# Keeping the first batch's u only transposed, and ending on column halves of the last chunk: an attention and mixer kernel on one core

## The chip, the cores and the metric

One core of a Trainium2 chip. The metric is the device time of one execution in microseconds (us). A profiled execution has a span, from first to last instruction record, some 1.8 us shorter than its device time; "span" below always means that one. All executions that are compared here counted as fast. A few of them, of the kernel before too, still took 1 to 4 us more than the rest; the two of which a trace was taken (named below) show TensorE at half clock for some 7 us near the beginning. Medians are quoted for that reason.

## The reference

Eight batches. Attention of 8 heads over 576 tokens of width 64, causal by blocks of 64; its output x has 512 columns. A mixer follows: token mixing with a hidden width of 256, then channel mixing with a hidden width of 1536.

```python
x = attention(q, k, v).transpose(0, 2, 1, 3).reshape(B, S, H * D)   # 8 x 576 x 512
xt = x.transpose(0, 2, 1)
h = np.maximum(xt @ w_tok1, 0.0) @ w_tok2
u = x + h.transpose(0, 2, 1)
h2 = np.maximum(u @ w_ch1, 0.0) @ w_ch2
return (u + h2).astype(np.float32)
```

## The kernel before

Work is handed to a planner: each `P.add(engine, cost, emit, deps, prio)` is one operation, and the planner simulates the engines and fixes the order on each by priorities and estimated readiness. So a change in one place moves instructions elsewhere. Matmul outputs live in four banks named `mm`; attention scores have two double banks of their own, `sc`. `EVAC` means "VectorE or ScalarE, as the planner likes".

The 576 tokens of a batch are four chunks of 128 rows and one of 64. The 64-row chunks of two batches share one "mixed" chunk (`um`). u is made in row layout, and is also needed transposed (uT) as the channel-up matmuls' moving operand. The first batch gets its uT directly, by a separate function, early; its u in row layout is then computed a second time, only because the output needs it:

```python
    def token_mix(b, x_done, w1_ready, w2_ready):
        # ... for b == 0 uT comes from first_uT(...)
        for si in range(5):
            # emit: two matmuls of 512 columns, w2_sb against aT       (L782)
            op = P.add("PE", mm_cost(512, 2), emit, ..., take=[(BANK, bank)])
            # emit: u = bank + x, or um for si == 4                     (L803)
            op = P.add("DVE", dve_cost(512), emit, [op], prio, give=[bank])
            u_done.append(op)
```

Channel-down makes the output chunk by chunk, and a last mixed chunk of its own kind ends the kernel:

```python
    def last_down(gt, ut, deps, prio):
        bank = {}
        def emit(o):
            nc.tensor.matmul(out=bank_of(bank), lhsT=ident, rhs=ut, start=True, stop=False)   # adds u
            for cc in range(NDC):                                                             # NDC = 12
                nc.tensor.matmul(out=bank_of(bank), lhsT=gt[:, cc, :], rhs=wc2_sb[:, cc, :],
                                 start=False, stop=(cc == NDC - 1))
        # ...
        for f, engine in enumerate(EVAC):          # one half of the columns on each engine, same bank
            def emit(o, f=f):
                cols = slice(256 * f, 256 * f + 256)
                cast(o, o_sb[oi][:, 0, cols], bank_of(bank)[:, cols])
            halves.append(P.add(engine, evac_cost(256)[engine], emit, [op] + o_war, prio))
        for kk in range(2):                        # 64 rows each, one on SyncE's queue, one on ScalarE's
            # dma_start(out=out[B - 2 + kk, 512:576, :], in_=o_sb[oi][64 * kk : 64 * kk + 64, 0, :])
            P.add(("SP", "ACT")[kk], 0.5, emit, halves, prio, xfer=4 * 0.086)

    def channel_down(b, g_done, wc2_ready, u_done, prio, mixed=False):
        # ... the last batch's mixed chunk: return last_down(...)
        for n, si in enumerate(chunks):
            for part in range(3):                  # four matmuls of 512 columns each
                deps = [prev] + (g_done + wc2_ready + u_done + o_war if part == 0 else [])
                # ...
            # VectorE: o_sb = bank + u ; every second chunk one store of 256 rows, 512 KB
```

The softmax here doesn't subtract the row's maximum and nothing guards it: scores larger than these inputs give would overflow.

## Time and profile before

| | before |
|---|---|
| device time, median of 6 (range) | 312.94 us (312.66 to 314.96) |
| span of the profiled execution | 311.63 us |
| first channel-up matmul starts | 29.89 us |
| last matmul ends | 306.30 us |
| last store issued | 307.20 us |
| its landing | 309.82 us |
| TensorE's idle time from 30 to 300 us | 1.49 us |

The middle rows come from the single records of the trace. Together they cut the span into parts that can be added: what comes before the first channel-up matmul, the middle up to the last matmul, and four steps of the end. The page, the chain, the groups and the order of time at the end are shown in the prediction. Two more views are used later. The first is the table by stretches, whose columns are the stretch, its length, the busy time (and instructions) of TensorE, its weight loads, VectorE, ScalarE and GpSimd, then clock, DMA share and GB/s:

```profile
40.00:50.00 10.00, 10.00 (x115) 5.03 (x112) 6.34 (x15) 6.48 (x8) 6.01 (x8) 1.00 1.25 200
60.00:70.00 10.00, 9.31 (x153) 5.39 (x152) 7.51 (x16) 6.87 (x11) 1.65 (x4) 1.00 1.40 182
```

TensorE has no gap at all from 40 to 50 us, and 0.69 us of gap from 60 to 70. The second is the list of stores issued after 305.5 us (tile, engine, count, size, median us from issue to landing):

```profile
out_dram<-o_sb SPq DMA_DIRECT2D x1, 128.0 KB, 2.3
out_dram<-o_sb ACTq DMA_DIRECT2D x1, 128.0 KB, 2.6
```

### The profile page before, as it was taken

How to read it: one execution, taken by the hardware profiler on the slowest of the kernel's cores; microseconds unless marked ns; L12 is line 12 of the kernel's file. 1: busy time of each engine (PE TensorE's matmuls, PEld its weight loads, DVE VectorE, ACT ScalarE, POOL GpSimd, SP SyncE). 2: the span in 40 equal slices, each digit the busy share in tenths (PEclk: the TensorE clock that was granted, in tenths of full speed). 3: DMA queues.
4: the chain of work that ended last, by engine and by line, in shares of the span. 5: the costliest groups of instructions: out<-in, count | busy, mean ns of one | idle time of the engine just before them, and what ended most of it. 6: DMA issues, size and time to landing. Idle time of an engine off the chain costs nothing.

```text
span 311.6 us, 7140 instructions
## 1 busy us (share of the span) xinstructions
PE 302.3 (97%) x3010; PEld 154.7 (50%) x3010; DVE 159.4 (51%) x377; ACT 164.8 (53%) x234; POOL 63.1 (20%) x96
## 2 busy tenths in 40 slices
PE   8999999999999999999999999999999999999993
PEld 3574436455465554554554555544444644444641
DVE  6868748598795495678375644452033021011021
ACT  5885862769756746677655475315505404604400
POOL 7956435711611501500400000000000000000000
PEclk9999999999999999999999999999999999999998
DMA  7999999997993996971690112114311313011013
GB/s 234 195 197 207 222 210 183 223 186 106 123 168 56 145 152 141 143 47 33 64 135 33 38 30 40 69 67 53 67 67 68 69 67 103 0 67 68 2 67 102
DMA packets 56864, 33.13 MB, mean 106 GB/s; under 512 B 43840, under 2 KB 47296, under 8 KB 56832
## 3 DMA queue, kind: packets, MB, share of 16 engines
q0 software_dynamic: 36960, 18.52, 45.5%
q1 hardware_dynamic: 19504, 13.44, 16.7%
q10 hardware_dynamic: 368, 0.72, 0.6%
q8 instruction: 23, 0.38, 0.5%
q14 instruction: 9, 0.07, 0.1%
HBM read 35.85 MB, written 9.44 MB: 145 GB/s over the span
## 4 chain that ended last, share of the span: by engine, by line
PE 83%; DMA 5%; DVE 5%; POOL 3%; issue 2%; ACT 0%; POOLq 0%
PE mm L979 29%; PE mm L874 27%; PE sc L460 7%; PE mm L507 7%; PE mm L688 5%; PE mm L782 4%; PE mm L901 4%; DMA qraw<-in_q_dram 3%; DMA kraw<-in_k_dram 2%; DVE x_sb L535 1%; DVE u_sb L803 1%; POOL gT L378 1%; PE mm L931 1%; POOL wc_sb L416 1%; POOL w_sb L397 1%
## 5 line engine op out<-in xcount | busy, mean ns | idle before, releaser
L479 ACT ACTIVATE e_sb<-sc 128x1024 bf16<-128x1024 f32 x95 | 92.5, 1027 | 37.7 <-PE sc L460 36.8
L979 PE MATMUL mm<-wc_sb,gT 128*128 128x512 bf16 x384 | 89.1, 379 | 0.0
L874 PE MATMUL mm<-uT,wc_sb 128*128 128x512 bf16 x384 | 88.4, 379 | 0.2 <-DVE x_sb L535 0.2
L674 ACT ACTIVATE gT<-mm 128x512 bf16<-128x512 f32 x74 | 44.2, 597 | 60.4 <-PE mm L874 60.3
L995 DVE TENSOR_TENSOR o_sb<-mm,u_sb 128x512 f32<-128x512 f32 x32 | 22.1, 690 | 87.1 <-PE mm L979 87.0
L874 PEld LDWEIGHTS <-wc_sb 128*128 128x128 bf16 x384 | 36.2, 98 | 45.3 <-issue 4.0
L979 PEld LDWEIGHTS <-gT 128*128 128x128 bf16 x384 | 35.3, 98 | 42.5 <-issue 4.3
L460 PE MATMUL sc<-qT,kT 32*128 32x320 bf16 (+4 forms) x744 | 35.9, 281 | 0.9 <-DVE qT L349 0.8
L507 PEld LDWEIGHTS <-e_sb 128*128 128x128 bf16 x896 | 31.1, 97 | 9.6 <-issue 4.6
L507 PE MATMUL mm<-v,e_sb 128*128 128x65 bf16 x896 | 33.2, 193 | 1.4 <-DVE uT L852 0.7
L378 POOL DMA_DIRECT2D v<-in_v_dram x30 | 25.4, 866 | 30.5 <-PE mm L507 27.9
L535 DVE TENSOR_TENSOR x_sb<-mm,rinv 128x320 bf16<-128x320 f32 x64 | 30.5, 489 | 1.4
L803 DVE TENSOR_TENSOR u_sb<-mm,x_sb 128x512 bf16<-128x512 f32 x32 | 20.1, 684 | 8.9 <-PE mm L782 8.1
L676 DVE TENSOR_SCALAR gT<-mm 128x512 bf16<-128x512 f32 x22 | 15.1, 688 | 15.3 <-PE mm L874 15.3
L460 PEld LDWEIGHTS <-kT 32*128 32x128 bf16 x752 | 12.7, 93 | 19.8 <-issue 17.0
L349 DVE STREAM_TRANSPOSE kT<-kraw 128x576 int32<-128x576 int32 (+1 forms) x20 | 20.1, 1033 | 4.5 <-PE sc L460 3.4
L349 DVE STREAM_TRANSPOSE qT<-qraw 128x576 int32<-128x576 int32 (+1 forms) x20 | 19.9, 1020 | 0.8 <-DMA qraw<-in_q_dram 0.5
L782 PE MATMUL mm<-aT,w_sb 128*128 128x512 bf16 x80 | 19.2, 379 | 0.0
L688 PE MATMUL mm<-x_sb,w_sb 128*128 128x512 bf16 (+1 forms) x102 | 17.9, 316 | 0.3 <-DVE x_sb L535 0.3
L674 ACT ACTIVATE aT<-mm 128x512 bf16<-128x512 f32 (+1 forms) x17 | 9.3, 547 | 16.7 <-PE mm L688 16.5
L329 POOL DMA_DIRECT2D kraw<-in_k_dram x15 | 8.4, 563 | 42.2 <-DVE kT L349 29.9
L485 DVE MEMSET e_sb<- 64x128 uint32 (+1 forms) x72 | 10.6, 153 | 11.2 <-ACT e_sb L479 8.0
(70 smaller groups left out, 183.9 us busy)
## 6 DMA issues: line engine op xcount, KB each, us to landing
out_dram<-o_sb SPq DMA_DIRECT2D x16, 512.0 KB, 2.8
kraw<-in_k_dram POOLq DMA_DIRECT2D x15, 288.0 KB, 6.6
qraw<-in_q_dram POOLq DMA_DIRECT2D x15, 288.0 KB, 7.7
v<-in_v_dram POOLq DMA_DIRECT2D x24, 128.0 KB, 5.3
wc_sb<-in_moe_w_ch_dram POOLq DMA_DIRECT2D x8, 192.0 KB, 8.0
wc_sb<-in_moe_w_ch_dram POOLq DMA_DIRECT2D x3, 512.0 KB, 10.7
gT<-in_v_dram POOLq DMA_DIRECT2D x9, 128.0 KB, 6.2
gT<-in_v_dram POOLq DMA_DIRECT2D x4, 256.0 KB, 12.9
```

The lines of the kernel that those rows point to most:

```text
L349: nc.vector.transpose(dst[:, 0:S, :] .rearrange("p s e -> p (s e)") .bitcast(I32) .rearrange("p (a k) -> p k a", k=NB)[:, k0:k1], raw2.bit ...
L378: nc.gpsimd.dma_start(out=dst, in_=src)
L460: nc.tensor.matmul(out=home(n)[:, c0 : c0 + w], lhsT=kT[i][r, j0 : j0 + 128, par], rhs=qT[i][r, i0 : i0 + w, par], start=(par == 0), stop= ...
L479: nc.scalar.activation(dst, sc[SC.index(note["pool"])][:, :, 0:n], EXP, scale=scale)
L507: nc.tensor.matmul(out=u[:, I, 0:65], lhsT=w, rhs=vt[:, J, head, 0:65], start=(J == 0), stop=(J == I),)
L535: nc.vector.tensor_tensor(out=xt[:, :, 64 * head : 64 * head + 64], in0=u[:, :, 0:64], in1=ri.to_broadcast([128, 5, 64]), op=MULT,)
L674: nc.scalar.activation(dst, src, RELU)
L688: nc.tensor.matmul(out=bank_of(bank)[:, w * n : w * n + w], lhsT=wt[:, 128 * tt : 128 * (tt + 1)], rhs=xt[:, c, cols], start=(c == 0), sto ...
L782: nc.tensor.matmul(out=bank_of(bank), lhsT=w2_sb[:, t, c0 : c0 + 128], rhs=at[:, t, :], start=(t == 0), stop=(t == NDT - 1),)
L803: nc.vector.tensor_tensor(out=dst, in0=bank_of(bank)[r, :], in1=xt[r, si, :], op=ADD)
L874: nc.tensor.matmul(out=bank_of(bank), lhsT=wc1_sb[:, m, 128 * cc : 128 * (cc + 1)], rhs=uT[b % 2][:, :, m, :], start=(m == 0), stop=(m == ...
L979: nc.tensor.matmul(out=bank_of(bank), lhsT=gt[:, cc, c0 : c0 + 128], rhs=wc2_sb[:, cc, :], start=(cc == 0), stop=(cc == NDC - 1),)
```

## The change

Two ideas. The first batch's row-layout u for its four full chunks isn't computed; in channel-down each output bank is opened by four 128-column matmuls that turn uT back (uT as weights, the identity as moving operand), the twelve ordinary ones accumulate on top, and the addition becomes a plain copy that either engine may do. At the end, the mixed chunk becomes an ordinary one and goes ahead of the last batch's regular chunks; the third regular chunk is stored by itself, and the fourth is computed, added and stored in two column halves, each in its own bank. On the way the wait for a free output tile moved from the matmuls to the evacuation.

```diff
-        for si in range(5):
+        for si in range(4 if b == 0 else 0, 5):
...
-    def last_down(gt, ut, deps, prio):          # all of it goes
...
+        turned = b == 0 and not mixed
+            last = b == B - 1 and n == 3
+            paired = not mixed and not (b == B - 1 and n >= 2)
+            for cols in (slice(0, 256), slice(256, 512)) if last else (slice(0, 512),):
...
+                        for m in range(NDM) if turned and part == 0 else ():
+                            nc.tensor.matmul(out=ps[:, 128 * m : 128 * (m + 1)],
+                                lhsT=uT[b % 2][:, si, m, :], rhs=ident, start=(m == 0), stop=False)
                         for cc in range(4 * part, 4 * part + 4):
-                            nc.tensor.matmul(out=bank_of(bank), ..., rhs=wc2_sb[:, cc, :], start=(cc == 0), ...)
+                            nc.tensor.matmul(out=ps, ..., rhs=wc2_sb[:, cc, cols], start=(cc == 0 and not turned), ...)
-                deps = [prev] + (g_done + wc2_ready + u_done + o_war if part == 0 else [])
+                    deps = [prev] + (g_done + wc2_ready + u_done if part == 0 else [])
...
+                    if turned:
+                        cast(o, dst, ps)
+                    else:
+                        nc.vector.tensor_tensor(out=dst, in0=ps, in1=..., op=ADD)
+                if not mixed and not paired:
+                        nc.sync.dma_start(out=out[b, c0 : c0 + 128, cols], in_=o_sb[oi][:, n % 2, cols])
...
+            if p == B - 1:       # after the mixed chunk, whose priority is now 10 * p + 3.9
+                channel_down(p, g_done, wc2_ready, u_done, 10 * p + 4)
```

More of the change, by code (lines that the diff above doesn't have):

```diff
@@ L858, in token_mix @@
         if not odd:
-            um_first[pair] = [u_done[4]]
+            um_first[pair] = [u_done[-1]]
         return done, um_done, u_done
@@ L922 @@
     out_n = [0]
-    def last_down(gt, ut, deps, prio):
-        bank = {}
-        def emit(o):
-            nc.tensor.matmul(out=bank_of(bank), lhsT=ident, rhs=ut, start=True, stop=False)
-            for cc in range(NDC):
-                nc.tensor.matmul(
-                    out=bank_of(bank),
-                    lhsT=gt[:, cc, :],
-                    rhs=wc2_sb[:, cc, :],
-                    start=False,
-                    stop=(cc == NDC - 1),
-                )
-        op = P.add(
-            "PE", mm_cost(512, NDC + 1), emit, deps + pads["ident"], prio, take=[(BANK, bank)]
-        )
-        oi = out_n[0] % 3
-        o_war = reuse(("o", oi))
-        halves = []
-        for f, engine in enumerate(EVAC):
-            def emit(o, f=f):
-                cols = slice(256 * f, 256 * f + 256)
-                cast(o, o_sb[oi][:, 0, cols], bank_of(bank)[:, cols])
-            halves.append(P.add(engine, evac_cost(256)[engine], emit, [op] + o_war, prio))
-        for kk in range(2):
-            def emit(o, kk=kk):
-                queue = nc.sync if o.engine == "SP" else nc.scalar
-                queue.dma_start(
-                    out=out[B - 2 + kk, 512:576, :],
-                    in_=o_sb[oi][64 * kk : 64 * kk + 64, 0, :],
-                )
-            P.add(("SP", "ACT")[kk], 0.5, emit, halves, prio, xfer=4 * 0.086)
     def channel_down(b, g_done, wc2_ready, u_done, prio, mixed=False):
@@ L964, in channel_down @@
         ut = um_sb[b // 2 % 2] if mixed else u_sb[b % 3]
-        if mixed and b == B - 1:
-            return last_down(gt, ut, g_done + wc2_ready + u_done, prio)
+        turned = b == 0 and not mixed
+        prev = None
         for n, si in enumerate(chunks):
-            bank = {}
-            prev = None
+            c0 = 0 if mixed else 128 * si
+            last = b == B - 1 and n == 3
+            paired = not mixed and not (b == B - 1 and n >= 2)
             if n % 2 == 0:
@@ L974, in channel_down @@
                 halves = []
-            c0 = 0 if mixed else 128 * si
-            for part in range(3):
-                def emit(o, part=part, c0=c0, bank=bank):
-                    for cc in range(4 * part, 4 * part + 4):
-                        nc.tensor.matmul(
-                            out=bank_of(bank),
-                            lhsT=gt[:, cc, c0 : c0 + 128],
-                            rhs=wc2_sb[:, cc, :],
-                            start=(cc == 0),
-                            stop=(cc == NDC - 1),
-                        )
-                deps = [prev] + (g_done + wc2_ready + u_done + o_war if part == 0 else [])
-                prev = P.add(
-                    "PE", mm_cost(512, 4), emit, deps, prio + 0.1 * n - 0.01 * part,
-                    take=[(BANK, bank)] if part == 0 else (),
-                )
@@ L992, in channel_down @@
-            reads(("gm", b // 2 % 2) if mixed else ("g", b % 2), prev)
-            def emit(o, si=si, oi=oi, n=n, bank=bank):
-                nc.vector.tensor_tensor(
-                    out=o_sb[oi][:, n % 2, :],
-                    in0=bank_of(bank),
-                    in1=ut if mixed else ut[:, si, :],
-                    op=ADD,
-                )
-            op = P.add("DVE", dve_cost(512), emit, [prev] + u_done, prio, give=[bank])
-            reads(("um", b // 2 % 2) if mixed else ("u", b % 3), op)
@@ L1004, in channel_down, with emit @@
-            halves.append(op)
+            for cols in (slice(0, 256), slice(256, 512)) if last else (slice(0, 512),):
+                width = cols.stop - cols.start
+                bank = {}
+                if paired or mixed:
+                    prev = None
+                for part in range(3):
+                    def emit(o, part=part, si=si, c0=c0, cols=cols, width=width, bank=bank):
+                        ps = bank_of(bank)[:, 0:width]
+                        for m in range(NDM) if turned and part == 0 else ():
+                            nc.tensor.matmul(
+                                out=ps[:, 128 * m : 128 * (m + 1)],
+                                lhsT=uT[b % 2][:, si, m, :],
+                                rhs=ident,
+                                start=(m == 0),
+                                stop=False,
+                            )
+                        for cc in range(4 * part, 4 * part + 4):
+                            nc.tensor.matmul(
+                                out=ps,
+                                lhsT=gt[:, cc, c0 : c0 + 128],
+                                rhs=wc2_sb[:, cc, cols],
+                                start=(cc == 0 and not turned),
+                                stop=(cc == NDC - 1),
+                            )
+                    deps = [prev] + (g_done + wc2_ready + u_done if part == 0 else [])
+                    cost = mm_cost(width, 4) + (mm_cost(128, 4) if turned and part == 0 else 0)
+                    prev = P.add(
+                        "PE", cost, emit, deps, prio + 0.1 * n - 0.01 * part + cols.start * 1e-4,
+                        take=[(BANK, bank)] if part == 0 else (),
+                    )
+                reads(("gm", b // 2 % 2) if mixed else ("g", b % 2), prev)
+                if turned:
+                    reads(("uT", b % 2), prev)
+                def emit(o, si=si, oi=oi, n=n, cols=cols, width=width, bank=bank):
+                    dst, ps = o_sb[oi][:, n % 2, cols], bank_of(bank)[:, 0:width]
+                    if turned:
+                        cast(o, dst, ps)
+                    else:
+                        nc.vector.tensor_tensor(
+                            out=dst, in0=ps, in1=(ut if mixed else ut[:, si, :])[:, cols], op=ADD
+                        )
+                op = P.add(
+                    EVAC if turned else "DVE", evac_cost(width), emit, [prev] + u_done + o_war, prio, give=[bank]
+                )
+                reads(("um", b // 2 % 2) if mixed else ("u", b % 3), op)
+                halves.append(op)
+                if not mixed and not paired:
+                    def emit(o, oi=oi, n=n, c0=c0, cols=cols):
+                        nc.sync.dma_start(out=out[b, c0 : c0 + 128, cols], in_=o_sb[oi][:, n % 2, cols])
+                    P.add("SP", 0.5, emit, [op], prio, xfer=8 * 0.086 * width / 512)
@@ L1013, in channel_down @@
                     reads(("o", oi), P.add("SP", 0.5, emit, halves, prio, xfer=4 * 0.086))
-            elif n % 2 == 1:
+            elif paired and n % 2 == 1:
                 def emit(o, oi=oi, i0=128 * (n - 1)):
@@ L1047 @@
             g_done = channel_up(p, uT_done, wc1_ready, 10 * p + 2)
-            channel_down(p, g_done, wc2_ready, u_done, 10 * p + 4)
+            if p < B - 1:
+                channel_down(p, g_done, wc2_ready, u_done, 10 * p + 4)
             if p % 2 == 1:
                 gm_done = channel_up_mixed(p // 2, um_done, wc1_ready, 10 * p + 3.5)
-                channel_down(p, gm_done, wc2_ready, u_done, 10 * p + 5, mixed=True)
+                prio = 10 * p + (5 if p < B - 1 else 3.9)
+                channel_down(p, gm_done, wc2_ready, u_done, prio, mixed=True)
+            if p == B - 1:
+                channel_down(p, g_done, wc2_ready, u_done, 10 * p + 4)
     with tc.manual_schedule():
```

## The prediction

> **What bounds the kernel now.** I read the page first (engines, slices, groups), then the chain of waits, the table by stretches of 10 us, the waits of TensorE, and last the order of time of the final 10 us.
>
> ```profile
> span 311.6 us, 7140 instructions
> PE 302.3 (97%) x3010; PEld 154.7 (50%) x3010; DVE 159.4 (51%) x377; ACT 164.8 (53%) x234; POOL 63.1 (20%) x96
> PE   8999999999999999999999999999999999999993
> PEclk9999999999999999999999999999999999999998
> GB/s 234 195 197 207 222 210 183 223 186 106 123 168 56 145 152 141 143 47 33 64 135 33 38 30 40 69 67 53 67 67 68 69 67 103 0 67 68 2 67 102
> ```
>
> TensorE has work in 97% of the span, in every slice but the first and last, at full clock. The 9.3 us in which it has none (311.6 - 302.3) split, by the stretches of 10 us, into 2.15 us before 20 us, 1.86 us between 20 and 300 us, and 5.3 us after the last matmul. So time comes off in three ways only: fewer columns through TensorE, fewer of those 1.86 us, or a shorter end. The loads are busy for the first 70 us, where VectorE is also most loaded: it is there that an earlier TensorE could run into something.
>
> The price of a matmul is read from the chain of waits, where long runs stand without a gap (start us, us, what), not from the mean durations of the groups, which overlap:
>
> ```profile
> 223.02 10.36 PE mm L979 x48
> 243.74 2.68 PE mm L901 x48
> ```
>
> 512 columns: 10.36 / 48 = 0.216 us each. 128 columns: 2.68 / 48 = 0.056 us each. The groups, with shapes kept apart, give the other durations (us busy, then mean ns of one):
>
> ```profile
> L782 PE MATMUL mm<-aT,w_sb 128*128 128x512 bf16 x80 | 19.2, 379 | 0.0
> L835 PE MATMUL mm<-ident,u_sb 128*128 128x128 bf16 x16 | 1.3, 220 | 0.0
> L803 DVE TENSOR_TENSOR u_sb<-mm,x_sb 128x512 bf16<-128x512 f32 x32 | 20.1, 684 | 8.9 <-PE mm L782 8.1 <-issue 0.8
> L995 DVE TENSOR_TENSOR o_sb<-mm,u_sb 128x512 f32<-128x512 f32 x32 | 22.1, 690 | 87.1 <-PE mm L979 87.0
> ```
>
> Last, the end, in order of time:
>
> ```profile
> 303.33 0.38 PE L929 MATMUL mm<-um_sb,ident 128*128 128x512 bf16 x1
> 303.55 2.75 PE L931 MATMUL mm<-wc_sb,gmT 128*128 128x512 bf16 x12
> 303.59 0.69 DVE L995 TENSOR_TENSOR o_sb<-mm,u_sb 128x512 f32<-128x512 f32 x1 [0.17 <-PE mm L979]
> 306.33 0.37 ACT L309 COPY o_sb<-mm 128x256 f32<-128x256 f32 x1 [12.57 <-PE mm L931]
> 306.74 0.42 DVE L311 COPY o_sb<-mm 128x256 f32<-128x256 f32 x1 [2.46 <-ACT o_sb L309]
> 307.19 0.47 SPq L954 DMA_DIRECT2D out_dram<-o_sb  x1
> 307.20 0.55 ACTq L954 DMA_DIRECT2D out_dram<-o_sb  x1
> ```
>
> The kernel meant the two copies to run side by side on two engines; they run one after the other, 0.86 us from the first start to 307.19. Both stores wait for both. From their issue to the end of the span it is 311.6 - 307.19 = 4.4 us.
>
> **What the Trainium skill says.** (1) "TensorE: Matmul & The Clock Gate", section "Back-to-back issue gap", gives N/2.4 + 2.5 ns for warm back-to-back matmuls, but also says that real streams of weight load and matmul settle elsewhere: about 81 ns at 128 columns and 131 ns at 512. This trace sides with the formula: 0.056 and 0.216 us, weight loads included, so the trace's numbers are used. (2) "PSUM — Partial Sum Buffer", section "Terms", says that two engines on one bank and quadrant at once is an error, reads against reads included. That is why the two end copies, halves of one bank, are kept apart: VectorE's shows an idle time ended by ScalarE. The changed kernel gives each column half its own bank. (3) "DMA: Bandwidth & Descriptors", section "Anatomy of one DMA — SWDGE (gpsimd) path", puts a nearly constant 2.0 us on a transfer, mostly the write's receipt. Written for another issuing path, it fits here: 128 KB stores issued from SyncE take a median of 2.4 us to land. So the end cannot fall much below its 4.4 us by moving fewer bytes.
>
> **The change, part by part.**
>
> First batch. The four 128-row chunks of u in row layout are no longer computed: 4 x 2 = 8 matmuls of 512 columns go, 8 x 0.216 = 1.73 us of TensorE, and 4 additions on VectorE of 0.684, 2.7 us. In exchange each output bank is opened by four matmuls of 128 columns, the transposed u against the identity: 16 x 0.056 = 0.89 us. They use the accumulation that the bank does anyway, so nothing else is added. Net on TensorE: -0.84 us. The four output additions (0.69 on VectorE) become plain copies; in the changed program's order one lies on VectorE and three on ScalarE (0.60 each, by the mean of ScalarE's 128x512 evictions), so VectorE loses 4 x 0.684 + 3 x 0.69 = 4.8 us of work between 28 and 70 us, and ScalarE gains 1.8.
>
> End. The mixed chunk goes in among the regular ones as an ordinary chunk: 12 matmuls as before, without the one that added u by the identity: -0.22 us. Its two stores go out some microseconds before the end. The last regular chunk is 24 matmuls of 256 columns, which at half of 0.216 each is the same 2.6 us. After the last matmul there is one 256-column addition on VectorE; at the 0.42 us of the 256-column copy, against 0.86 for the two in a row: -0.43 us. Then one store of 128 KB in rows of 1 KB in place of two of 128 KB. The end's 256 KB showed 133 and 129 GB/s in the two microseconds from 308 us, so about 2 us of moving; half of that with the fixed part unchanged I put at -0.2 us, an estimate, not -1.
>
> Waits between 20 and 300 us. The largest is this:
>
> ```profile
> PE mm L507 <- DVE uT L852: 0.7, 1, 0.7
> ```
>
> It is at 67.6 us: VectorE, behind four additions, a fifth and a transpose, empties a bank late. In the changed order four transpose matmuls and four of the output's stand between that point and the attention of the next batch, and VectorE carries less. I expect this wait to go, and something smaller to come elsewhere: -0.4 us of the 1.86, with an error as large as that.
>
> Sum: -0.84 - 0.22 - 0.43 - 0.2 - 0.4 = -2.1 us. From the median of 312.9: **310.8 us**, 0.7% faster.
>
> **The rivals.**
>
> A. The loads set the pace early, and what TensorE saves is waited away. For it: some 200 GB/s (195 to 234 by slice) through the first 45 us; GpSimd waits there for landings of weights and v; the second batch's last cast of v ends at 47.05 us and attention on TensorE starts at 48.26, only 1.2 us later, while the change moves TensorE forward by 1.73 - 0.45 = 1.28 us by then (eight of the sixteen small matmuls come earlier). Against it: VectorE's casts at 45.59 us came after a fill that waited for ScalarE's exponentials, not for a load, and that fill moves forward too. If v lands no earlier, 0.1 to 1 us is lost: 311 to 312 us.
>
> B. The scheduler's new order makes new bank waits. The order of all instructions differs from 28 us on, and a bank that waits for the last of several evictions on one engine costs 0.2 to 0.7 us each time, as it does at 68 and 70 us in this trace. Three extra copies on ScalarE stand ahead of exponentials around 50 to 70 us, where it is 41% to 85% busy by stretch. Two or three such waits would cost 1 us: 311.5 to 312. Against it: the waits are few even where VectorE is 88% busy, and that load falls.
>
> C. The bigger prize: VectorE's relief in the crowded stretch takes out nearly all of the 1.86 us, and the store at the end shrinks by a full microsecond: 308.8. Against it: the fixed part of a store, and most of the waits lying outside the first two batches' output.
>
> D. The end grows: four stores now leave SyncE in the last few microseconds, and the last ones queue behind a 512 KB one. Against it: before, 512 KB issued at 304.31 was moved by 307. In the new order the 512 KB leave about 1.5 us sooner, and the two halves' stores are 1.3 us apart, twice an issue. I give it +0.3 us at most.
>
> **Range and chances.** Only the 1.06 us of TensorE work are nearly sure. Each of the other terms could fail by its own size, rival A and B can cost 1 us together, C can give 1.5, and the three runs before spread from 312.66 to 314.96. So 309.5 to 312.4 should hold it 8 times in 10. Over 2% faster means below 306.7, more than TensorE's columns, all its waits and any shortening of the end that I can argue for add up to: 2%. Over 2% slower would need 6 us of new waits: 2%. Within 2%: 96%.
>
> **What would show it.** TensorE's busy time falls from 302.3 to about 301.2. The new identity matmuls are 16, of 128 columns, and the group of u against w_sb falls from 80 to 72. In the waits of TensorE, the 0.7 us for uT is gone and the sum from 20 to 300 us is about 1.5 us; well over 2 is rival B, and waits for casts of v or for transposes of q and k near 46 us are rival A. At the end, one VectorE addition of 0.42 us lies between last matmul and last store, and last matmul to end of span is about 4.7 us in place of 5.3. The prediction is wrong in kind if TensorE gains its 1.06 us and the time stays at 312.9: the saving was then waited away in the first 70 us, or the clock fell.

## The result, and the profile after

Changed kernel: 310.74 us median of 6 (310.42 to 311.1); before, in the same rounds, 312.94. Ratio 0.9921, interval [0.9898, 0.9944]. Ratios here are the mean time of one kernel's fast runs over that of the other's of the same rounds, so not quite the ratio of the medians that are quoted. 310.8 had been predicted. The agreement is worth little by itself: the parts of the sum have to be compared.

The page of the changed kernel:

```profile
span 309.2 us, 7176 instructions
PE 300.4 (97%) x3029; PEld 155.4 (50%) x3029; DVE 157.6 (51%) x372; ACT 165.8 (54%) x235; POOL 63.1 (20%) x96
PE   7999989999999999999999999999999999999995
PEclk9999999999999999999999999999999999999999
```

TensorE lost 1.9 us of busy time. Its columns account for 1.06; another 0.9 lie before 20 us (17.84 us busy by the stretches, then 16.93), ahead of anything that changed: the sixteen matmuls of zeros with which both kernels begin took 6.04 us in the one execution and 5.00 in the other, and TensorE then waited for the first transposed q in both, 0.40 and 1.21 us. A row of slices is too coarse to show where the time went. Groups by shape, and two pieces of the chain of waits, confirm that the work is what the diff says:

```profile
L782 PE MATMUL mm<-aT,w_sb 128*128 128x512 bf16 x72 | 17.0, 380 | 0.0
L950 PE MATMUL mm<-ident,uT 128*128 128x128 bf16 x16 | 1.6, 220 | 0.0
L803 DVE TENSOR_TENSOR u_sb<-mm,x_sb 128x512 bf16<-128x512 f32 x28 | 17.4, 683 | 6.7 <-PE mm L782 6.7
```

```profile
43.84 0.22 PE mm L950 x4
44.06 1.73 PE mm L958 x8
```

72 for 80 matmuls, 16 small ones at 0.22 / 4 = 0.055 us each, four additions fewer on VectorE. The same stretches as shown for before:

```profile
40.00:50.00 10.00, 9.15 (x112) 4.89 (x113) 5.54 (x14) 5.84 (x7) 6.14 (x8) 1.00 1.24 199
60.00:70.00 10.00, 9.46 (x139) 5.89 (x132) 9.13 (x19) 6.64 (x11) 2.02 (x4) 1.00 1.47 156
```

A gap of 0.85 us now stands between 40 and 50 us, where there was none, and the 0.69 from 60 to 70 only fell to 0.54. VectorE is *busier* from 60 to 70 than before. And the end, in order of time, with the store that is issued last:

```profile
298.82 7.10 PE L958 MATMUL mm<-wc_sb,gT 128*128 128x512 bf16 x44
304.12 2.63 SPq L992 DMA_DIRECT2D out_dram<-o_sb  x3
304.65 0.43 DVE L981 TENSOR_TENSOR o_sb<-mm,u_sb 128x256 f32<-128x256 f32 x1 [0.56 <-PE mm L958]
305.96 0.42 DVE L981 TENSOR_TENSOR o_sb<-mm,u_sb 128x256 f32<-128x256 f32 x1 [0.88 <-PE mm L958]
```

```profile
out_dram<-o_sb SPq DMA_DIRECT2D x1, 128.0 KB, 1.7
```

Here is the cut of the span for both, and what was predicted for each part (us):

| part | before | after | difference | predicted |
|---|---|---|---|---|
| up to the first channel-up matmul | 29.89 | 28.08 | -1.81 | -1.73 (8 matmuls) |
| from there to the last matmul's end | 276.41 | 277.84 | +1.43 | +0.89 - 0.22 - 0.4 = +0.27 |
| last matmul to last store's issue | 0.90 | 0.49 | -0.41 | -0.43 |
| issue to landing | 2.63 | 1.70 | -0.93 | -0.2, with the next row |
| landing to end of span | 1.81 | 1.12 | -0.69 | |
| sum | 311.63 | 309.23 | -2.40 | -2.1 |

The middle row contains +0.89 for the sixteen small matmuls and -0.22 for the identity matmul. TensorE's idle time from 30 to 300 us, by the stretches, rose from 1.49 to 2.06 us, +0.57. That leaves about 0.2. Missing records aren't the reason: 3010 and 3029 matmuls differ by just what the diff says, -8 + 16 - 1 + 12. It may lie inside the waits, whose cost the idle time understates, since the records of matmuls overlap (one of 512 columns is 0.38 us long, and the next starts 0.216 after it): the wait at 42.01 us shows 0.71 of idle time, but 0.91 from start to start. The trace doesn't settle it. So two terms of the prediction are off, by about +1 and -1.4 us, and almost cancel. The experiments are about these two.

### The profile page after: what moved, and what is told of

The parts are those of the page before. It is cut to its first block, busy times and chain, and to the rows that moved or that the text cites. A ratio compares the mean times of both kernels' runs of the same rounds, so it can differ in the third digit from the quotient of the medians.

```text
span 309.2 us, 7176 instructions
## 1 busy us (share of the span) xinstructions
PE 300.4 (97%) x3029; PEld 155.4 (50%) x3029; DVE 157.6 (51%) x372; ACT 165.8 (54%) x235; POOL 63.1 (20%) x96
## 4 chain that ended last, share of the span: by engine, by line
PE 85%; DMA 5%; DVE 4%; POOL 3%; ACT 1%; issue 1%; POOLq 0%
PE mm L958 30%; PE mm L874 26%; PE sc L460 8%; PE mm L507 7%; PE mm L782 5%; PE mm L688 5%; PE mm L901 4%; DMA qraw<-in_q_dram 3%; DMA kraw<-in_k_dram 2%; DVE x_sb L535 1%; ACT e_sb L479 1%; POOL gT L378 1%; DVE qT L349 1%; DVE kT L349 1%; POOL wc_sb L416 1%
## 5 line engine op out<-in xcount | busy, mean ns | idle before, releaser
L958 PE MATMUL mm<-wc_sb,gT 128*128 128x512 bf16 (+1 forms) x396 | 89.6, 373 | 0.0
L981 DVE TENSOR_TENSOR o_sb<-mm,u_sb 128x512 f32<-128x512 f32 (+1 forms) x29 | 19.5, 672 | 85.8 <-PE mm L958 85.8
L958 PEld LDWEIGHTS <-gT 128*128 128x128 bf16 x396 | 36.7, 98 | 41.3 <-issue 3.6
L803 DVE TENSOR_TENSOR u_sb<-mm,x_sb 128x512 bf16<-128x512 f32 x28 | 17.4, 683 | 6.7 <-PE mm L782 6.7
L782 PE MATMUL mm<-aT,w_sb 128*128 128x512 bf16 x72 | 17.0, 380 | 0.0
L529 DVE RECIPROCAL rinv<-mm 128x5 f32<-128x5 f32 x64 | 10.6, 180 | 9.2 <-PE mm L507 9.0
```

Source lines behind the costliest of these rows:

```text
L782: nc.tensor.matmul(out=bank_of(bank), lhsT=w2_sb[:, t, c0 : c0 + 128], rhs=at[:, t, :], start=(t == 0), stop=(t == NDT - 1),)
L958: nc.tensor.matmul(out=ps, lhsT=gt[:, cc, c0 : c0 + 128], rhs=wc2_sb[:, cc, cols], start=(cc == 0 and not turned), stop=(cc == NDC - 1),)
L981: nc.vector.tensor_tensor(out=dst, in0=ps, in1=(ut if mixed else ut[:, si, :])[:, cols], op=ADD)
```

## The experiments

Twelve runs, all with correct results. Medians are in us; "before" in the three calls had 313.15, 313.17 and 313.27. In each of the first two, one run of before took over 316 us, which widens the intervals and pulls the ratios down a little.

### Each part alone

The changed end with the first batch as it was:

```diff
 # from the changed kernel
-        for si in range(4 if b == 0 else 0, 5):
+        for si in range(5):
-        turned = b == 0 and not mixed
+        turned = False
```

> The changed kernel with its new end, but the first batch as in the kernel before; TensorE's order is that of the kernel before up to the last 64 of its instructions. As predicted, the end is worth 0.22 us of TensorE (no identity matmul) + 0.43 us (one eviction in place of two in a row) + 0.2 us (store) = 0.85 us: 312.1 us, ratio 0.997. By the profiles of before and after, last matmul to end of span fell by 2.0 us and not by 0.63: then the end alone is worth 0.22 + 2.0 = 2.2 us: 310.7 us, ratio 0.993, all of the measured gain.

Measured: 310.9 (310.67 to 311.38), ratio 0.9918 [0.9885, 0.995].

The first batch as changed, with the end as it was:

```diff
 # from the changed kernel: last_down is back, and is called for the last mixed chunk
-            last = b == B - 1 and n == 3
-            paired = not mixed and not (b == B - 1 and n >= 2)
+            last = False
+            paired = not mixed
 # the calls of channel_down, with their priorities, as before
```

> The changed kernel's first batch with the end of the kernel before; the order is that of the changed kernel up to the end. As predicted, 0.84 us of TensorE columns and 0.4 us of waits are saved: 1.24 us, 311.7 us, ratio 0.996. The profile of after shows 2.04 us of TensorE waits between 27 and 300 us where before had 1.50, so by it the part is worth 0.84 - 0.54 = 0.3 us: 312.6 us, ratio 0.999. Rival: the 0.84 us show in full (312.1) if the longer waits are one profile's chance.

Measured: 312.9 (312.51 to 313.54), ratio 0.9984 [0.9953, 1.0014].

The end is worth 313.15 - 310.9 = 2.25 us, nearly everything; the first batch 0.25, not to be told from nothing. They had been predicted at 0.85 (0.22 + 0.43 + 0.2) and 1.24 (0.84 + 0.4). In the trace of the end alone the middle is 276.19 us, 0.22 less than before's: that is the identity matmul and nothing else. In that of the first batch alone it is 278.04, 1.63 longer, against 1.78 gained up to the first channel-up matmul (29.89 - 28.11).

### Why the store landed earlier

Three differences lie between 2.63 and 1.70 us: two stores of 64 rows became one of 128, half the bytes are left to move, and ScalarE's queue, whose store landed last, is no longer used. The last half's store was split by rows over both queues:

```diff
-                        nc.sync.dma_start(out=out[b, c0 : c0 + 128, cols], in_=o_sb[oi][:, n % 2, cols])
+                        # for the second column half: rows 0 to 63 from SyncE, 64 to 127 from ScalarE
+                        queue.dma_start(out=out[b, c0 + r0 : c0 + r1, cols], in_=o_sb[oi][r0:r1, n % 2, cols])
```

> The changed kernel, but the very last store (128 KB) is cut by rows into two of 64 KB, one issued from SyncE and one from ScalarE, as the kernel before did with its last two. If the end shrank because ScalarE's queue no longer carries a last store, 0.7 to 1.6 us come back: 311.5 to 312.3 us against 310.7, and the wait for the last landing grows from 0.6 us towards the 2.0 us of before. If it shrank because half the bytes are left to move, the time stays within 0.2 us of the changed kernel.

Measured: 311.61 (311.12 to 311.89), ratio 0.9937 [0.9908, 0.9967]. Its last stores:

```profile
out_dram<-o_sb SPq DMA_DIRECT2D x1, 64.0 KB, 2.0
out_dram<-o_sb ACTq DMA_DIRECT2D x1, 64.0 KB, 2.3
```

Each moves half the bytes of the changed kernel's single store, and each lands later. Is it ScalarE's queue? The whole store, from ScalarE:

```diff
-                    P.add("SP", 0.5, emit, [op], prio, xfer=8 * 0.086 * width / 512)
+                    P.add("ACT" if cols.start else "SP", 0.5, emit, [op], prio, xfer=8 * 0.086 * width / 512)
```

> The changed kernel with its very last store, whole with its 128 rows of 1 KB, issued from ScalarE and not from SyncE. In the run with two half stores the ScalarE one landed 2.28 us after its issue and the SyncE one 1.96, against 1.70 for the single one of 128 rows. If the queue of ScalarE is the slower one, this store lands after 2.0 us or more and the kernel takes 0.3 us more than the changed one (311.0). If stores of 64 rows are the slow thing, it lands after 1.7 to 1.8 us and the time stays.

Measured: 310.94 (310.85 to 311.32), ratio 0.992 [0.9884, 0.9956].

```profile
out_dram<-o_sb ACTq DMA_DIRECT2D x1, 128.0 KB, 1.7
```

1.73 us from ScalarE, 1.70 from SyncE: the queue is not the cause. Slow is the pair of half-height stores. The Trainium skill has that advice, in "DMA: Bandwidth & Descriptors", section "Rules for kernel authors": two transfers to disjoint partition halves serialize, and one transfer of 128 partitions should take their place. The traces agree: 1.70 us for one store of 128 KB, 2.28 for the later of two of 64 KB, 2.63 for the later of two of 128 KB. The packets of the two halves moved mostly one after the other, SyncE's from 307.58 to 308.03 us and ScalarE's from 307.87 to 308.31; those of the single store moved from 307.24 to 307.76. These 64-row stores also took 0.47 (SyncE) and 0.55 us (ScalarE) to issue, against 0.33 to 0.35 for 128 rows. A second store in the way isn't needed for the late landing: in the changed kernel itself the first of the mixed chunk's two stores (64 rows, 128 KB, issued at 299.80 us) had moved nearly all its packets before those of the second began, and still landed after 2.25 us.

Finally the last chunk in one piece, 512 columns and one 256 KB store:

```diff
-            last = b == B - 1 and n == 3
+            last = False
```

> The changed kernel with its last regular chunk whole: one bank, one addition of 512 columns, one store of 256 KB from SyncE with rows of 2 KB. Bytes theory: 0.27 us more for the addition (0.69 for 0.42) and 0.5 us more to land (2.2 us for 256 KB, 1.7 for the last 128 KB), or more: 311.5 us. Queue theory: only the addition and 0.1 us: 311.1 us.

Measured: 311.48 (311.35 to 312.22), ratio 0.9939 [0.9909, 0.9969].

```profile
out_dram<-o_sb SPq DMA_DIRECT2D x1, 256.0 KB, 2.1
```

2.12 us for 256 KB against 1.70 for 128 KB: 0.42 us for 128 KB. From last matmul to issue it took 0.76 instead of 0.49. The halves are thus worth some 0.7 us (0.27 + 0.42) of the 2.2. And of the 0.93 by which the landing came sooner, some 0.4 belong to the bytes (2.12 - 1.70) and 0.5 to the two stores of half height (2.63 - 2.12).

### What happens after the landing

0.69 us of the gain come after the last byte is down. At the end SyncE waits for each DMA completion semaphore in turn, by number, and then meets the other engines at a barrier. Records of the traces (us, semaphore), cut to this part:

```
before: 309.84 S109   309.90 S111   310.00 S112   310.07 S115   310.56 S116   310.65 S117   310.71 S118   drains, barrier to 311.58
after:  306.79 S106   307.28 S107   307.36 S109   307.43 S111   307.50 S112   308.13 S115   308.19 S116   308.25 S117   308.31 S118   drains, barrier to 309.18
```

Each step takes 0.06 to 0.1 us, except one pause of 0.49. Before, the last store was on semaphore 109, third in the list: all the later steps came after the landing, with the pause (310.07 to 310.56) among them. After, it is on 115, the pause (306.79 to 307.28) passes while the store is still under way, and three steps are left. If that is right, any change that shifts SyncE's instructions would do without touching the end. So the kernel before got its third batch's 512 KB stores as two of 256 KB each; that changes the order on SyncE alone, some 140 to 150 us before the end (not 200, as the expectation says):

```diff
 # from the kernel before
+            elif n % 2 == 1 and b == 2:
+                for kk in range(2):
+                    # dma_start(out=out[b, i0 + 128 * kk : i0 + 128 * kk + 128, :], in_=o_sb[oi][:, kk, :])
             elif n % 2 == 1:
```

> The kernel before, with nothing changed but that two of its sixteen 512 KB stores, those of the third batch, each go out as two of 256 KB: SyncE has two more stores to issue, 200 us before the end, and the completion semaphores of its later stores are two places further on. Theory: of the 2.0 us that the end lost, about 0.67 are neither eviction nor landing but what SyncE has left to do after the last landing (1.79 us before, 1.12 after): the waits still to be stepped through in their fixed order, and one pause of 0.49 us in SyncE's instructions, whose place depends on how many of them there are. Then this kernel gains 0.4 to 0.7 us, 312.3 to 312.6 against 313.0, ratio 0.998, and the time from last landing to end of span is about 1.1 to 1.3 us. Rival: those 0.67 us belong to the two last stores on two queues; then nothing moves: ratio 1.000, and 1.8 us from landing to end.

Measured: 312.89 (312.49 to 313.02), ratio 0.9976 [0.9935, 1.0016]. The time moved by 0.28 us, less than the 0.4 to 0.7 expected and within the interval; the trace is clearer. The pause ran from 307.83 to 308.31, before the landing, the last store sat on 112, and landing to end took 1.20 us instead of 1.81. The landing itself was later by 0.23 (2.86 against 2.63), so the net in the trace is 0.38. The reading of the steps holds. The place of the pause is settled too: in all fourteen kept traces SyncE's 79th record, counted from the start, is followed by a gap of 0.45 us or more, whether that record is a step of the end, a store or a wait before one. So the count of its instructions sets where the pause falls. Why SyncE pauses there stays open.

### Two banks for the two copies

The prediction said that the two end copies run in a row because they share a bank. The kernel before, with its last chunk in two banks of 256 columns:

```diff
 # from the kernel before, last_down
-        bank = {}
+        bank, bank2 = {}, {}
 # the identity matmul and the twelve others become pairs of 256 columns, one per bank
-                cast(o, o_sb[oi][:, 0, cols], bank_of(bank)[:, cols])
+                cast(o, o_sb[oi][:, 0, cols], bank_of((bank, bank2)[f])[:, 0:256])
```

> The kernel before, its last chunk in two accumulation banks of 256 columns in place of one of 512, so that VectorE and ScalarE copy from a bank each. If the shared bank kept the copies apart, they now start within 0.1 us of each other, the stores go out 0.45 us after the last matmul in place of 0.89, and the kernel gains 0.4 us: 312.6 against 313.0, ratio 0.9987. Rival: the order of the two has another cause (VectorE waits for ScalarE for a buffer or a semaphore); then they stay one after the other and nothing is gained.

Measured: 312.8 (312.33 to 314.85), ratio 0.9984 [0.9946, 1.0022]; by medians -0.37 us.

```profile
305.61 0.42 DVE L311 COPY o_sb<-mm 128x256 f32<-128x256 f32 x1 [1.98 <-PE mm L935]
305.72 0.37 ACT L309 COPY o_sb<-mm 128x256 f32<-128x256 f32 x1 [12.60 <-PE mm L935]
306.12 0.47 SPq L958 DMA_DIRECT2D out_dram<-o_sb  x1
```

Both copies now wait for the matmul alone and overlap. From last matmul to issue it takes 0.44 us, not 0.90; landing and steps are as before (2.63, 1.80). The interval of the times doesn't exclude nothing; the trace shows the 0.46.

### The first batch's new waits

Why did a net 0.84 us of matmuls buy only some 0.25? In order of time, the changed kernel around 40 us, TensorE and one row of ScalarE, and its two next largest waits (start us, us, engine, line; in brackets the idle time before and what ended it):

```profile
39.36 0.63 PE L460 MATMUL sc<-qT,kT 32*128 32x512 bf16 x8
39.92 1.04 PE L874 MATMUL mm<-uT,wc_sb 128*128 128x512 bf16 x4
40.02 1.94 ACT L479 ACTIVATE e_sb<-sc 128x1024 bf16<-128x1024 f32 x2
41.10 0.21 PE L460 MATMUL sc<-qT,kT 32*128 32x64 bf16 x2
...
42.01 0.63 PE L460 MATMUL sc<-qT,kT 32*128 32x64 bf16 x14 [0.71 <-ACT e_sb L479]
...
50.61 0.58 PE L507 MATMUL mm<-v,e_sb 128*128 128x65 bf16 x14 [0.21 <-DVE x_sb L535]
...
67.70 0.58 PE L507 MATMUL mm<-v,e_sb 128*128 128x65 bf16 x14 [0.35 <-DVE x_sb L535]
```

and the kernel before in the same place:

```profile
39.43 0.63 PE L460 MATMUL sc<-qT,kT 32*128 32x512 bf16 x8
40.00 2.77 PE L874 MATMUL mm<-uT,wc_sb 128*128 128x512 bf16 x12
42.69 0.64 PE L460 MATMUL sc<-qT,kT 32*128 32x64 bf16 x16
```

The second batch's scores need a score bank that ScalarE's exponentials must empty first, two of them in 1.94 us. Before, twelve channel-up matmuls stood between two score sets. Because channel-up now starts 1.8 us earlier, only four are left for this place, and TensorE has run out of work: channel-down can't start, as its first part waits for all twelve `g_done`, the last of them done at 41.69 us (the weights, which the next expectation blames, had landed by 40.1). If lack of filling is the cause, a channel-down part that depends only on its own four slices of gT gives filling. For all batches:

```diff
 # from the changed kernel
-                    deps = [prev] + (g_done + wc2_ready + u_done if part == 0 else [])
+                    deps = [prev] + (g_done[4*part : 4*part+4] if len(g_done) == NDC else g_done[part : part+1]) \
+                        + [wc2_ready[part]] + (u_done if part == 0 else [])
```

> The changed kernel, but each third of an output chunk waits, in the plan that orders the instructions, only for its own third of gT and of the second channel weights, not for all of both. In the changed kernel TensorE waits 0.71 us at 41 us for exponentials: it had run out of other work, since the plan let no output matmul start before the last third of the weights, which lands at about 40.9 us. Now eight identity matmuls and eight output matmuls stand before those scores. If that is the cause, the 0.7 us go and the kernel is at 310.1 us, ratio 0.990. Rival: the loads or VectorE make it wait at the next place (v at 46 us, transposes of q and k): then TensorE's waits between 20 and 80 us stay at about 2.1 us in all, and the time at 310.7.

Measured: 311.95 (311.53 to 315.25), ratio 0.9974 [0.9928, 1.002]. Its profiled execution had half clock from 12 to 18 us, so the parts after it are compared only in their lengths: middle 278.78 us, longer, not shorter. The same for the first batch alone, to leave the order of the others:

```diff
 # as above, but only where `turned` is true; otherwise the changed kernel's line
```

> The changed kernel, but the plan lets each third of the first batch's output chunks wait for its own third of gT and second channel weights only; the other batches are planned as in the changed kernel. With that rule for all batches the wait at 41 us went and others of 0.84, 0.39, 0.34 and 0.31 us came, and first channel matmul to last matmul grew from 277.84 to 278.78 us. If the batches after the first were at fault, this kernel has 277.2 us there and 310.2 in all. If filling the wait at 41 us only moves it to where VectorE is behind, around 50 to 80 us, it has 278.5 or more, and 311.5 in all.

Measured: 312.01 (311.52 to 312.12), ratio 0.9957 [0.9945, 0.9968]; the changed kernel 310.83. Middle 278.70 us.

```profile
55.08 0.58 PE L507 MATMUL mm<-v,e_sb 128*128 128x65 bf16 x14 [0.38 <-DVE x_sb L535]
65.40 0.38 PE L835 MATMUL mm<-ident,u_sb 128*128 128x128 bf16 x4 [0.34 <-DVE um_sb L803]
70.84 1.46 PE L874 MATMUL mm<-uT,wc_sb 128*128 128x512 bf16 x6 [0.84 <-DVE x_sb L535]
```

The gap at 42 us is gone, and others stand at 55, 65 and 71 us, ended by VectorE; a smaller one of 0.23 at 66 us is ScalarE's. The version for all batches has the same gaps, each 3.1 us later by its slow start. My theory that this gap was the loss fell: filling it moves the wait to where VectorE is behind. Until 70 us TensorE runs against what the other engines hand it, so that work taken from it there is mostly waited away. That this holds for any order is not shown: besides the changed kernel's own, only these two were tried.

### Finer still

The changed kernel again:

> The changed kernel itself, as the measure for the others of this call: 310.7 to 310.9 us, ratio 0.992; 1.7 us from the last store's issue to its landing and 1.1 from there to the end of the span.

Measured: 310.83 (310.67 to 311.2), ratio 0.9923 [0.991, 0.9936].

The second column half cut into two of 128 columns:

```diff
-            for cols in (slice(0, 256), slice(256, 512)) if last else (slice(0, 512),):
+            for cols in (slice(0, 256), slice(256, 384), slice(384, 512)) if last else (slice(0, 512),):
```

> The changed kernel, its last chunk in column pieces of 256, 128 and 128 in place of two of 256. The last addition should take about 0.29 us and not 0.42 (512 columns take 0.69, 256 take 0.42), the last store has 64 KB in rows of 512 bytes: 0.1 us less to move, or nothing less. Expected gain over the changed kernel 0.15 to 0.3 us: 310.5. Rival: one more store on SyncE moves its pause of 0.49 us behind the last landing; then it is lost again and more: 311.0.

Measured: 312.49 (311.91 to 314.0), ratio 0.9979 [0.9963, 0.9996]: a miss, 1.7 us slower than the changed kernel where 0.15 to 0.3 faster had been expected. The profiled execution had half clock from 18 to 25 us; its end is undisturbed:

```profile
306.62 2.82 SPq L992 DMA_DIRECT2D out_dram<-o_sb  x4
...
308.49 0.29 DVE L981 TENSOR_TENSOR o_sb<-mm,u_sb 128x128 f32<-128x128 f32 x1 [0.38 <-PE mm L958]
```

The last addition shrank to 0.29 us and ended at 308.78, but the store was only issued at 309.11: SyncE's pause fell right there. From last matmul to end it takes 3.77 us, against 3.31 in the changed kernel; that is 0.5 of the 1.7, and what the other 1.2 are no trace shows. And 64 KB in rows of 512 bytes took 2.08 us to land, longer than 128 KB in rows of 1 KB. The same with the third batch's stores in 256 KB, so as to move the pause:

```diff
 # finer_end, and for b == 2 two stores of 128 rows in place of each of 256
```

> The same with the third batch's two 512 KB stores as four of 256 KB, so that the last store's completion semaphore is the last of those that SyncE steps through at the end (three steps of 0.07 us fewer are left after the landing than in the changed kernel, two fewer than in the one with the finer end). If the steps left after the landing count, landing to end of span falls from 1.12 to 0.95 us or less and the kernel is 0.15 us under the one with the finer end: 310.35. Rival: these waits cost nothing, the same time as the finer end.

Measured: 311.43 (310.63 to 312.03), ratio 0.9938 [0.9925, 0.9951]. A miss as well (310.35 expected). The pause has left the end, for a place where SyncE waits for an addition anyway: last matmul to issue 0.53, landing 1.71, landing to end 0.91 with the store on semaphore 118, the last. Its profiled execution (310.76) is as good as the changed kernel's; the other five lie at 310.63 to 312.03. So it is not better, and what makes it scatter is open. It also casts doubt on rows of 512 bytes as the cause of the 2.08 us: they landed in 1.71 here. None of the other eleven beats the changed kernel.

## Why the prediction was right, and where it wasn't

The time was right, by a sum in which two terms were wrong with opposite signs. That they nearly cancelled was luck.

- **TensorE's columns, -0.84 and -0.22: right.** The eight matmuls show as -1.81 at the first channel-up matmul (1.73, the rest chance), the small ones run at 0.055 us each, and the end alone shortens the middle by exactly 0.22.
- **Last matmul to store, -0.43: right**, -0.41. Its reason, the shared bank, was tested by the kernel with two banks and holds. It is what the page on PSUM, named in the prediction, leads one to expect.
- **The store, -0.2: mis-sized.** It measured -1.6. The prediction took the time to land as a fixed part plus bytes, and "the fixed part unchanged" was the failing step: two stores of half height against one of full height account for 0.93 (some 0.4 of it the bytes), and SyncE's steps after the landing, which the prediction had not separated from the store at all, for 0.69. It named a store shrunk "by a full microsecond" under rival C and refused it. The trace of before had a warning: the seven 128 KB stores whose median of 2.4 us seemed to confirm the fixed part are all of 64 rows, and the one planned has 128.
- **The waits, -0.4: wrong in sign.** They rose by 0.57 us. The wait of 0.69 for uT did go, as argued; what came elsewhere was larger: 0.71 at 42 us, then 0.21 and 0.35 for attention's evacuation, and 0.44 in four small gaps from 41 to 64 us; after 70 us there is 0.45 less than before. This is rival B, though not in its predicted form: the largest wait was no output bank behind ScalarE's extra copies but a score bank with too little work in front of it. The prediction's own mark for it, a sum from 20 to 300 us well over 2, was met: 2.44, from 1.86. VectorE's relief of 4.8 us didn't show as idle time either: from 30 to 70 us it was busy 28.32 us after 29.18, since work for later batches moved forward into it, 1.7 us of transposes of q and k among it.
- **Rival A: not seen.** No wait for a cast of v came up near 46 us. **Rival D: not seen.** The last store was issued at 306.41, as soon as its addition ended (306.38).
- **A misreading.** ScalarE's 85% is that of 70 to 80 us; from 50 to 70, which rival B speaks of, the stretches give 41% and 69%. Nothing in the sum rests on it.
- **The marks.** "About 4.7 us" from last matmul to end was 3.31. TensorE's busy time, predicted at 301.2, was 300.4, lower by what differed before 20 us.

## What to carry to other kernels

At the very end of a kernel, every step in series counts in full: give the last evacuation a bank and an engine to itself, and send one store over all 128 partitions, neither two of half the rows nor the whole width. Where other engines pace TensorE, as in this kernel's crowded first 70 us, matmuls taken away can come back as waits; ask what will fill the time in which the next stage waits, before counting the columns. And when a prediction comes out right, measure each part alone anyway: here one half was worth 2.25 us and the other 0.25, where 0.85 and 1.24 had been put.

## What the Trainium skill lacked or had wrong

- "DMA: Bandwidth & Descriptors": its fit of a nearly constant 2.0 us plus bytes is for GpSimd's path; a store of 128 KB over 128 partitions from SyncE or ScalarE landed in 1.70 and 1.73 us, less than that constant, and one of 256 KB in 2.12. A fit for these two issuers is lacking.
- The same page says not to split by partition halves, without a price. Here the later of two half-height stores landed after 2.28 us (64 KB) and 2.63 us (128 KB), against 1.70, and each took 0.47 to 0.55 us to issue against 0.33 to 0.35.
- No page that I found describes what follows the last landing inside the span: SyncE's steps through the completion semaphores (0.06 to 0.1 us each), a pause of 0.49 us after its 79th record, and a barrier, 0.91 to 1.81 us in all, by which semaphore the last store has and where the pause falls.
- "TensorE: Matmul & The Clock Gate": its figures for real streams, 81 ns at 128 columns and 131 ns at 512, fit neither of the durations here, 55 to 56 and 216 ns; the formula in the same section does.
